# A grouped 1x1 convolution limited by transfers: splitting its relief chunks into two partition-offset variants with buffers and queues of their own

## The chip, the cores and the metric

One core of one Trainium2 chip. The time is that of the device, in microseconds, from many executions. Executions of the kernel before spread from 513.6 to 527.6 us over all rounds, 2.7% from the fastest to the slowest, so comparisons are made between runs of the same rounds on the same chip. A "ratio" below is the mean time of one kernel's fast runs over the mean of the other's fast runs of the same rounds, so it is not quite the ratio of the medians that are quoted beside it. Verdicts are at 2%: a change under 2% is called "same".

## The reference

```python
H = W = 512; G = 4; Cg = 48; C = 192; k = 1        # x: (1, 512, 512, 192) bf16, w: (1, 1, 4, 48, 48) bf16
xg = x.reshape(B, H, W, G, Cg)
out = einsum('bhwgc,gcd->bhwgd', xg, w[0, 0])       # four independent 48x48 products for each pixel
```

262,144 pixels of 384 bytes are read and as many written: 201.3 MB. That is nearly all there is to pay for.

## The kernel before

Pixels are cut into chunks. A natural chunk gives 32 pixels to each of 128 partitions (one partition's share is one run of 12,288 bytes). Four pixels of each partition make a group: TensorE transposes it (six transposes), VectorE copies the result out of PSUM, TensorE multiplies it with a block weight (six matmuls), ScalarE and VectorE copy the product to an output buffer. SyncE issues loads, ScalarE issues stores.

Every fourth chunk is a "relief" chunk of 120 partitions. Its store is issued from GpSimd, behind a tiny transfer of one partition:

```python
RPARTS = 120
nparts = [128 if k == "nat" else RPARTS for k in kinds]
...
# GpSimd, for a relief chunk
gp.dma_start(scratch[0:1, 2 * nd + 1:2 * nd + 2], scratch[0:1, 0:1]).then_inc(dm_sem, 16)
gp.dma_start(rows_view(of, n), o_sb[b][0:RPARTS, 0:F]).then_inc(ra_sem[b], 16)
...
# SyncE, for every chunk: 128 partitions, also for the 120 of a relief chunk
src = xf[chunk_pix0[n]:chunk_pix0[n] + 128 * sizes[n], :].rearrange("(p i) c -> p (i c)", p=128)
sp.dma_start(x_sb[b][:, 0:sizes[n] * C], src).then_inc(ld_sem[b], 16)
```

The plan behind it: a store of 120 partitions is to leave one of the core's sixteen DMA engines without work, and the tiny transfer is to see to it that it is the same one each time. For the first half the trace speaks: each of the sixteen relief stores has sixteen completion marks, one of them 2.8 to 10.4 us ahead of the next (3.1 us against 9.4 and later for the store issued at 398.86 us). Which engine that is, and whether it is always the same, no view shows; that was assumed. Five load buffers and six store buffers serve both kinds of chunk.

## Time and profile before

| | before |
|---|---|
| median time, 4 runs known at the start | 522.45 us (519.64 to 527.58) |
| TensorE busy | 81% |
| bytes moved, mean rate | 203.83 MB, 388 GB/s |
| a load of 128 partitions, issue to landing | 32.8 us |
| TensorE's waits for loads | 88.1 us in 37 waits |

The lines of the page, and how they are read, stand in the prediction below.

### The profile page before, as it was taken

How to read it: one execution, taken by the hardware profiler on the slowest of the kernel's cores; microseconds unless marked ns; L12 is line 12 of the kernel's file. 1: busy time of each engine (PE TensorE's matmuls, PEld its weight loads, DVE VectorE, ACT ScalarE, POOL GpSimd, SP SyncE). 2: the span in 40 equal slices, each digit the busy share in tenths (PEclk: the TensorE clock that was granted, in tenths of full speed). 3: DMA queues.
4: the chain of work that ended last, by engine and by line, in shares of the span. 5: the costliest groups of instructions: out<-in, count | busy, mean ns of one | idle time of the engine just before them, and what ended most of it. 6: DMA issues, size and time to landing. Idle time of an engine off the chain costs nothing.

```text
span 525.6 us, 14096 instructions
## 1 busy us (share of the span) xinstructions
PE 426.9 (81%) x6250; PEld 417.4 (79%) x6250; DVE 352.2 (67%) x677; ACT 351.9 (67%) x521; POOL 18.1 (3%) x41
## 2 busy tenths in 40 slices
PE   4999938499894978989598598977978597887894
PEld 4999937499884977988498597977977596887793
DVE  2788917378673865868477386874867575676783
ACT  2698826468683874868477396874867575776784
POOL 1000000000000000000000000000000000000000
PEclk9999969789897997989989798997999989999999
DMA  8999999999999999999999999999999999999986
GB/s 296 420 396 421 335 419 387 402 401 388 427 398 393 399 392 408 367 415 423 401 403 373 397 354 382 427 403 417 370 423 419 406 412 371 422 351 393 339 311 249
DMA packets 21229, 203.83 MB, mean 388 GB/s; under 512 B 3120, under 2 KB 4144, under 8 KB 5168
## 3 DMA queue, kind: packets, MB, share of 16 engines
q1 hardware_dynamic: 10432, 102.26, 47.5%
q10 hardware_dynamic: 7920, 77.07, 35.9%
q0 software_dynamic: 2816, 23.60, 13.9%
q8 instruction: 49, 0.80, 0.6%
q14 instruction: 12, 0.10, 0.1%
HBM read 102.25 MB, written 100.66 MB: 386 GB/s over the span
## 4 chain that ended last, share of the span: by engine, by line
DMA 66%; PE 31%; SPq 0%; issue 0%; ACT 0%; ACTq 0%
DMA x_sb<-in_x_dram 66%; PE o_ps L279 17%; PE xT_ps L257 15%; SPq L227 0%; ACT o_sb L337 0%; SPq L222 0%; ACTq L322 0%; ACTq L38 0%
## 5 line engine op out<-in xcount | busy, mean ns | idle before, releaser
L304 DVE COPY xT_sb<-xT_ps 128x768 bf16<-128x768 bf16 x520 | 288.1, 555 | 159.2 <-PE xT_ps L257 157.6
L337 ACT CAST o_sb<-o_ps 128x768 bf16<-128x768 f32 x364 | 281.9, 800 | 123.3 <-PE o_ps L279 123.0
L257 PE MATMUL xT_ps<-ident,x_sb 128*128 128x128 bf16 x3120 | 274.9, 227 | 88.9 <-DMA x_sb<-in_x_dram 88.1
L279 PE MATMUL o_ps<-wt,xT_sb 128*128 128x144 bf16 (+1 forms) x3120 | 317.6, 241 | 0.0
L257 PEld LDWEIGHTS xT_ps<-ident,x_sb 128*128 128x128 bf16 x3120 | 211.2, 102 | 97.6 <-DMA x_sb<-in_x_dram 95.6
L279 PEld LDWEIGHTS o_ps<-wt,xT_sb 128*128 128x128 bf16 x3120 | 234.3, 102 | 0.6 <-ACT o_sb L337 0.2
L333 ACT CAST o_sb<-o_ps 128x384 bf16<-128x384 f32 x156 | 74.9, 480 | 43.6 <-PE o_ps L279 42.9
L312 DVE CAST o_sb<-o_ps 128x384 bf16<-128x384 f32 x156 | 86.2, 552 | 3.4 <-PE o_ps L279 2.6
L208 POOL DMA_DIRECT2D scratch<-scratch x16 | 8.3, 520 | 475.7 <-DVE xT_sb L304 421.2
L210 POOL DMA_DIRECT2D out_dram<-o_sb x16 | 8.6, 535 | 0.0
L299 DVE CAST wt<-o_ps 128x480 bf16<-128x480 f32 x1 | 0.7, 657 | 3.4 <-PE o_ps L240 3.4
L240 PE MATMUL o_ps<-w_sb,esel 48*128 48x48 bf16 x10 | 0.6, 210 | 2.8 <-DMA w_sb<-in_w_dram 2.8
L240 PEld LDWEIGHTS o_ps<-w_sb,esel 48*128 48x128 bf16 x10 | 0.5, 110 | 2.7 <-POOL esel L189 2.7
L337 ACT ACT_TABLE_LOAD x1 | 1.3, 1283 | 0.8 <-PEq L363 0.8
L189 POOL TENSOR_SCALAR_AFFINE_SELECT esel<-esel 48x272 bf16<-48x272 bf16 x1 | 0.4, 405 | 0.0
L185 POOL MEMSET esel<- 48x272 bf16 x1 | 0.3, 318 | 0.3 <-POOLq L363 0.3
L193 POOL TENSOR_SCALAR_AFFINE_SELECT ident<-ident 128x128 bf16<-128x128 bf16 x1 | 0.3, 290 | 0.0
L186 POOL MEMSET ident<- 128x128 bf16 x1 | 0.2, 198 | 0.0
L187 POOL MEMSET scratch<- 16x40 bf16 x1 | 0.1, 122 | 0.0
L363 POOL MEMSET const-float32-0.0<- 128x1 f32 x1 | 0.1, 99 | 0.3 <-issue 0.3
L363 POOL MEMSET const-bfloat16-1.0<- 128x1 bf16 x1 | 0.1, 103 | 0.0
L363 POOL MEMSET const-uint8-127<- 128x1 uint8 x1 | 0.1, 102 | 0.0
(1 smaller groups left out, 0.1 us busy)
## 6 DMA issues: line engine op xcount, KB each, us to landing
x_sb<-in_x_dram SPq DMA_DIRECT2D x63, 1536.0 KB, 32.8
out_dram<-o_sb ACTq DMA_DIRECT2D x47, 1536.0 KB, 15.4
out_dram<-o_sb POOLq DMA_DIRECT2D x16, 1440.0 KB, 16.2
x_sb<-in_x_dram SPq DMA_DIRECT2D x2, 768.0 KB, 20.4
out_dram<-o_sb ACTq DMA_DIRECT2D x2, 768.0 KB, 10.6
x_sb<-in_x_dram SPq DMA_DIRECT2D x4, 192.0 KB, 7.5
x_sb<-in_x_dram SPq DMA_DIRECT2D x2, 384.0 KB, 13.9
out_dram<-o_sb ACTq DMA_DIRECT2D x4, 192.0 KB, 7.0
```

What stands on the lines that cost most here:

```text
L189: gp.affine_select(out=esel[:], in_=esel[:], pattern=[[-1, ECOLS]], compare_op=AluOpType.is_equal, fill=0.0, base=ESHIFT, channel_multipli ...
L208: gp.dma_start(scratch[0:1, 2 * nd + 1:2 * nd + 2], scratch[0:1, 0:1]).then_inc(dm_sem, 16)
L210: gp.dma_start(rows_view(of, n), o_sb[b][0:RPARTS, 0:F]).then_inc(ra_sem[b], 16)
L240: last = pe.matmul(o_ps[:, NOB - 1, col:col + 48], lhsT=esel[:, s0:s0 + 128], rhs=w_sb[:, g, :], start=True, stop=True, skip_group_check=True)
L257: last = pe.transpose(xT_ps[:, g % NXP, j * 128:(j + 1) * 128], xb[:, col:col + 128], ident[:])
L279: last = pe.matmul(o_ps[:, v % NOB, c0:c1], lhsT=xs[:, j * 128:(j + 1) * 128], rhs=wt[:, WOFF[tc]:WOFF[tc] + (c1 - c0)], start=(tc == 0), ...
L299: dve.tensor_copy(wt[:], o_ps[:, NOB - 1, 0:WCOLS]).then_inc(dve_done, 1)
L304: dve.tensor_copy(xT_sb[g % NXS][:], xT_ps[:, g % NXP, 0:768]).then_inc(dve_done, 1)
L312: dve.tensor_copy(obuf(n)[:, u * UC:(u + 1) * UC], o_ps[:, v % NOB, 0:UC]).then_inc(dve_done, 1)
L333: ins = act.copy(ob[:, u * UC:(u + 1) * UC], o_ps[:, v % NOB, 0:UC])
L337: ins = act.copy(dst, o_ps[:, v % NOB:v % NOB + 2, 0:UC])
L363: nc = _bacc.Bacc("TRN2", target_bir_lowering=False, num_devices=1)
```

## The change

The intent: relieve DMA engines more, and with finer grain. There are two relief variants, each a range of partitions that does not start at zero: 60 partitions from 36, and 44 partitions from 52. Now their loads too go through GpSimd's queue, into relief buffers of their own, and each transfer has a one-partition or a five-partition transfer ahead of it, which was to decide which engines are relieved (the code's `move_cursor`; the recorded texts speak of the cursor). That such transfers steer anything was an assumption. There are 24 relief chunks instead of 16, so that 620 groups are computed, not 520. Because a relief range ends at partition 96, the transposes of a relief group use 96 rows, and rows below the range hold zeros. The diff, shortened:

```diff
-NBI=5, NBO=6, n_relief=16, first_relief=3, relief_gap=3
-RPARTS = 120
+NBI = 5; NBO = 5; NRI = 2; NRO = 2
+RELIEF = {"relA": (36, 60, 1), "relB": (52, 44, 5)}   # first partition, partitions, tiny transfer's partitions
+REND = 96
+B_EVERY = 4; N_RELIEF = 24; FIRST_RELIEF = 4; RELIEF_GAP = 2
...
+            def move_cursor(skip):
+                gp.dma_start(scratch[0:skip, 2 * nd + 1:2 * nd + 2], scratch[0:skip, 0:1]).then_inc(dm_sem, 16)
+            def load(n):
+                wait_in_free(wq, n)
+                ...
+                move_cursor(skip)
+                gp.dma_start(xr_sb[i][p0_:p0_ + rows, 0:sizes[n] * C], rows_view(xf, n)).then_inc(rl_sem[i], 16)
+            def store(n):
+                wait_evacuated(wq, n)
+                ...
+                move_cursor(skip)
+                gp.dma_start(rows_view(of, n), or_sb[i][p0_:p0_ + rows, 0:sizes[n] * C]).then_inc(rs_sem[i], 16)
...
-            for n in range(n_chunks):                      # SyncE
+            for n in nat_ids:
...
-  pe.transpose(xT_ps[:, g % NXP, j * 128:(j + 1) * 128], xb[:, col:col + 128], ident[:])
+  pe.transpose(xT_ps[:, g % NXP, j * 128:j * 128 + rows], xb[0:rows, col:col + 128], ident[0:rows, 0:rows])
...   (clearing of xr_sb and xT_sb at the start; the copies of relief groups take 96 of 128 columns)
```

More of the change, by code (lines that the diff above doesn't have):

```diff
@@ L7 @@
 F32 = mybir.dt.float32
-C = 192
+GROUPS = 4
+CG = 48
+C = GROUPS * CG
 UC = 2 * C
@@ L20 @@
 ECOLS = 272
+PPC = 32
+HEAD = (4, 4, 8, 16)
+TAIL = (16, 8, 4, 4)
+NBI = 5
+NBO = 5
+NRI = 2
+NRO = 2
 NOB = 5
@@ L24 @@
 LOOK = 2
-RPARTS = 120
+RELIEF = {"relA": (36, 60, 1), "relB": (52, 44, 5)}
+REND = 96
+RPPC = 32
+B_EVERY = 4
+N_RELIEF = 24
+FIRST_RELIEF = 4
+RELIEF_GAP = 2
+SHARE = (2, 4, 7)
+ST_DELAY = 1
 class Waiter:
@@ L38, in wait @@
         self.eng.wait_ge(sem, val)
-def _ints(v):
-    return tuple(int(t) for t in str(v).split("_") if t != "")
-def plan_chunks(npix, PPC, RPPC, n_relief, head, tail, first_relief, relief_gap):
-    assert npix % 128 == 0
-    rel_pix = RPARTS * RPPC
-    while n_relief > 0 and (npix - n_relief * rel_pix) % 512 != 0:
-        n_relief -= 1
-    cols = (npix - n_relief * rel_pix) // 128
-    if n_relief == 0 or cols < sum(head) + sum(tail) + PPC:
-        n_relief = 0
-        cols = npix // 128
-    if cols < sum(head) + sum(tail):
-        head, tail = (), ()
-    mid = cols - sum(head) - sum(tail)
-    nat = list(head)
-    while mid > 0:
-        s = min(PPC, mid)
-        nat.append(s)
-        mid -= s
-    nat += list(tail)
-    assert all(s % 4 == 0 for s in nat)
-    chunks = [("nat", s) for s in nat]
-    pos = first_relief
-    for r in range(n_relief):
-        pos = min(pos, len(chunks) - len(tail))
-        chunks.insert(pos, ("rel", RPPC))
-        pos += relief_gap + 1
-    return chunks
@@ L73, in bass_standalone__grouped__vision_kernel, with relief_kinds, plan_chunks @@
-def bass_standalone__grouped__vision_kernel(nc, x, w, out, PPC=32, NBI=5, NBO=6, head="4_4_8_16", tail="16_8_4_4",
-           share="2_4_7", n_relief=16, first_relief=3, relief_gap=3, st_delay=1, nat_ring="act"):
+def relief_kinds(n_relief):
+    return ["relB" if B_EVERY and i % B_EVERY == B_EVERY - 1 else "relA" for i in range(n_relief)]
+def plan_chunks(npix):
+    assert npix % 512 == 0, "the pixel count must be a multiple of 512"
+    for n_relief in range(N_RELIEF, -1, -1):
+        rk = relief_kinds(n_relief)
+        rest = npix - sum(RELIEF[k][1] * RPPC for k in rk)
+        if rest < 0 or rest % 512 != 0:
+            continue
+        cols = rest // 128
+        head, tail = list(HEAD), list(TAIL)
+        if cols < sum(head) + sum(tail) + PPC:
+            if n_relief:
+                continue
+            head, tail = [], []
+        mid = cols - sum(head) - sum(tail)
+        nat = head
+        while mid > 0:
+            nat.append(min(PPC, mid))
+            mid -= nat[-1]
+        nat += tail
+        chunks = [("nat", s) for s in nat]
+        pos = FIRST_RELIEF
+        for k in rk:
+            pos = min(pos, len(chunks) - len(tail))
+            chunks.insert(pos, (k, RPPC))
+            pos += RELIEF_GAP + 1
+        return chunks
+    raise AssertionError("no chunk plan")
@@ L75, in bass_standalone__grouped__vision_kernel @@
+def bass_standalone__grouped__vision_kernel(nc, x, w, out):
     B, H, W_, Cx = x.shape
-    assert Cx == C
+    assert Cx == C and tuple(w.shape) == (1, 1, GROUPS, CG, CG)
     npix = B * H * W_
-    head, tail, share = _ints(head), _ints(tail), set(_ints(share))
-    chunks = plan_chunks(npix, PPC, PPC, n_relief, head, tail, first_relief, relief_gap)
-    assert chunks[-1][0] == "nat"
+    chunks = plan_chunks(npix)
     n_chunks = len(chunks)
@@ L83, in bass_standalone__grouped__vision_kernel @@
     sizes = [c[1] for c in chunks]
-    assert all(s % 4 == 0 for s in sizes)
-    rel_ids = [n for n in range(n_chunks) if kinds[n] == "rel"]
+    nrows = [128 if k == "nat" else RELIEF[k][1] for k in kinds]
     nat_ids = [n for n in range(n_chunks) if kinds[n] == "nat"]
+    rel_ids = [n for n in range(n_chunks) if kinds[n] != "nat"]
     n_rel = len(rel_ids)
-    ordinal, cnt = {}, {"nat": 0, "rel": 0}
-    for n in range(n_chunks):
-        ordinal[n] = cnt[kinds[n]]
-        cnt[kinds[n]] += 1
-    nparts = [128 if k == "nat" else RPARTS for k in kinds]
+    ordinal = {n: i for ids in (nat_ids, rel_ids) for i, n in enumerate(ids)}
     xf = x.rearrange("b h w c -> (b h w) c")
@@ L100, in bass_standalone__grouped__vision_kernel @@
         chunk_pix0.append(p0)
-        p0 += nparts[n] * sizes[n]
+        p0 += nrows[n] * sizes[n]
     assert p0 == npix
@@ L110, in shared @@
     def shared(g):
-        return (g % 5 == 2) or ((g % 10) in share)
+        return (g % 5 == 2) or ((g % 10) in SHARE)
     dve_prog = [("wcopy", 0)]
@@ L123, in rows_view @@
     def rows_view(ap, n):
-        s = sizes[n]
-        return ap[chunk_pix0[n]:chunk_pix0[n] + nparts[n] * s, :].rearrange("(p i) c -> p (i c)", p=nparts[n])
+        rows, s = nrows[n], sizes[n]
+        return ap[chunk_pix0[n]:chunk_pix0[n] + rows * s, :].rearrange("(p i) c -> p (i c)", p=rows)
     with ExitStack() as es:
@@ L130, in bass_standalone__grouped__vision_kernel @@
         o_sb = [es.enter_context(nc.sbuf_tensor(f"o_sb{i}", [128, PPC * C], BF16)) for i in range(NBO)]
-        xT_sb = [es.enter_context(nc.sbuf_tensor(f"xT_sb{i}", [128, 768], BF16)) for i in range(NXS)]
+        xr_sb = [es.enter_context(nc.sbuf_tensor(f"xr_sb{i}", [128, RPPC * C], BF16)) for i in range(NRI)]
+        or_sb = [es.enter_context(nc.sbuf_tensor(f"or_sb{i}", [128, RPPC * C], BF16)) for i in range(NRO)]
+        xT_sb = [es.enter_context(nc.sbuf_tensor(f"xT_sb{i}", [128, 2 * UC], BF16)) for i in range(NXS)]
@@ L132, in bass_standalone__grouped__vision_kernel @@
         ident = es.enter_context(nc.sbuf_tensor("ident", [128, 128], BF16))
-        esel = es.enter_context(nc.sbuf_tensor("esel", [48, ECOLS], BF16))
-        w_sb = es.enter_context(nc.sbuf_tensor("w_sb", [48, 4, 48], BF16))
+        esel = es.enter_context(nc.sbuf_tensor("esel", [CG, ECOLS], BF16))
+        w_sb = es.enter_context(nc.sbuf_tensor("w_sb", [CG, GROUPS, CG], BF16))
         wt = es.enter_context(nc.sbuf_tensor("wt", [128, WCOLS], BF16))
-        scratch = es.enter_context(nc.sbuf_tensor("scratch", [16, 2 * max(n_rel, 1) + 8], BF16))
+        scratch = es.enter_context(nc.sbuf_tensor("scratch", [16, 4 * max(n_rel, 1) + 8], BF16))
@@ L137, in bass_standalone__grouped__vision_kernel, with sem @@
         xT_ps = es.enter_context(nc.psum_tensor("xT_ps", [128, NXP, 1024], BF16))
         o_ps = es.enter_context(nc.psum_tensor("o_ps", [128, NOB, 512], F32))
-        sem = lambda name: es.enter_context(nc.semaphore(name))
+        def sem(name):
+            return es.enter_context(nc.semaphore(name))
         ld_sem = [sem(f"ld{i}") for i in range(NBI)]
         st_sem = [sem(f"st{i}") for i in range(NBO)]
-        ra_sem = [sem(f"ra{i}") for i in range(NBO)]
-        dm_sem = sem("dm_sem")
@@ L145, in bass_standalone__grouped__vision_kernel @@
-        w_sem, id_sem, e_sem, p0_sem, p1_sem, sc_sem = (sem(n_) for n_ in ("w_sem", "id_sem", "e_sem", "p0_sem", "p1_sem", "sc_sem"))
-        wb_sem = sem("wb_sem")
-        t_done, mm_done, dve_done, act_done = sem("t_done"), sem("mm_done"), sem("dve_done"), sem("act_done")
+        rl_sem = [sem(f"rl{i}") for i in range(NRI)]
+        rs_sem = [sem(f"rs{i}") for i in range(NRO)]
+        z_sem = sem("z_sem")
+        zt_sem = sem("zt_sem")
+        w_sem, id_sem, e_sem, wb_sem = sem("w_sem"), sem("id_sem"), sem("e_sem"), sem("wb_sem")
@@ L150, in xbuf, with used_rows @@
+        p0_sem, p1_sem, sc_sem, dm_sem = sem("p0_sem"), sem("p1_sem"), sem("sc_sem"), sem("dm_sem")
+        t_done = sem("t_done")
+        mm_done = sem("mm_done")
+        dve_done = sem("dve_done")
+        act_done = sem("act_done")
         def xbuf(n):
-            return x_sb[n % NBI]
+            return x_sb[ordinal[n] % NBI] if kinds[n] == "nat" else xr_sb[ordinal[n] % NRI]
+        def used_rows(n):
+            return 128 if kinds[n] == "nat" else REND
         def obuf(n):
-            return o_sb[n % NBO]
@@ L156, in bass_standalone__grouped__vision_kernel, with wait_loaded @@
-        st_before, nat_c, rel_c = {}, [0] * NBO, [0] * NBO
-        for n in range(n_chunks):
-            st_before[n] = (nat_c[n % NBO], rel_c[n % NBO])
+            return o_sb[ordinal[n] % NBO] if kinds[n] == "nat" else or_sb[ordinal[n] % NRO]
+        def wait_loaded(wq, n):
+            k = ordinal[n]
             if kinds[n] == "nat":
-                nat_c[n % NBO] += 1
+                wq.wait(ld_sem[k % NBI], 16 * (k // NBI + 1))
             else:
-                rel_c[n % NBO] += 1
@@ L164, in wait_loaded @@
-        def wait_loaded(wq, n):
-            wq.wait(ld_sem[n % NBI], 16 * (n // NBI + 1))
+                wq.wait(rl_sem[k % NRI], 16 * (k // NRI + 1))
         def wait_in_free(wq, n):
-            if n >= NBI:
-                wq.wait(t_done, chunk_g1[n - NBI])
-        def wait_out_free(wq, n):
-            a_, r_ = st_before[n]
-            wq.wait(st_sem[n % NBO], 16 * a_)
-            wq.wait(ra_sem[n % NBO], 16 * r_)
+            k = ordinal[n]
+            if kinds[n] == "nat":
+                if k >= NBI:
+                    wq.wait(t_done, chunk_g1[nat_ids[k - NBI]])
+            elif k >= NRI:
+                wq.wait(t_done, chunk_g1[rel_ids[k - NRI]])
@@ L176, in wait_evacuated @@
+        def wait_out_free(wq, n):
+            k = ordinal[n]
+            if kinds[n] == "nat":
+                wq.wait(st_sem[k % NBO], 16 * (k // NBO))
+            else:
+                wq.wait(rs_sem[k % NRO], 16 * (k // NRO))
         def wait_evacuated(wq, n):
@@ L196, in _ @@
             gp.wait_ge(sc_sem, 1)
-            nd = 0
-            for n in range(n_chunks):
-                b = n % NBO
-                if kinds[n] == "nat" and nat_ring != "pool":
-                    continue
-                wait_evacuated(wq, n)
-                F = sizes[n] * C
-                if kinds[n] == "nat":
-                    if nat_ring == "pool":
-                        gp.dma_start(rows_view(of, n), o_sb[b][:, 0:F]).then_inc(st_sem[b], 16)
-                else:
-                    gp.dma_start(scratch[0:1, 2 * nd + 1:2 * nd + 2], scratch[0:1, 0:1]).then_inc(dm_sem, 16)
-                    nd += 1
-                    gp.dma_start(rows_view(of, n), o_sb[b][0:RPARTS, 0:F]).then_inc(ra_sem[b], 16)
@@ L211, in _ @@
-            for b in range(NBO):
-                if nat_c[b] and nat_ring == "pool":
-                    gp.wait_ge(st_sem[b], 16 * nat_c[b])
-                if rel_c[b]:
-                    gp.wait_ge(ra_sem[b], 16 * rel_c[b])
-            if nd:
-                gp.wait_ge(dm_sem, 16 * nd)
+            state = {"nd": 0}
+            def move_cursor(skip):
+                nd = state["nd"]
+                gp.dma_start(scratch[0:skip, 2 * nd + 1:2 * nd + 2], scratch[0:skip, 0:1]).then_inc(dm_sem, 16)
+                state["nd"] = nd + 1
@@ new lines, in load @@
+            def load(n):
+                wait_in_free(wq, n)
+                i = ordinal[n] % NRI
+                p0_, rows, skip = RELIEF[kinds[n]]
+                move_cursor(skip)
+                gp.dma_start(xr_sb[i][p0_:p0_ + rows, 0:sizes[n] * C], rows_view(xf, n)).then_inc(rl_sem[i], 16)
+            def store(n):
+                wait_evacuated(wq, n)
+                i = ordinal[n] % NRO
+                p0_, rows, skip = RELIEF[kinds[n]]
+                move_cursor(skip)
+                gp.dma_start(rows_view(of, n), or_sb[i][p0_:p0_ + rows, 0:sizes[n] * C]).then_inc(rs_sem[i], 16)
@@ new lines, in _ @@
+            for i in range(1, NRI if n_rel else 0, 2):
+                gp.memset(xr_sb[i][:], 0.0).then_inc(z_sem, 1)
+            if n_rel:
+                gp.wait_ge(z_sem, NRI)
+            for n in rel_ids[:NRI]:
+                load(n)
+            for k, n in enumerate(rel_ids):
+                store(n)
+                if k + NRI < n_rel:
+                    load(rel_ids[k + NRI])
+            for i in range(NRO):
+                cnt = len(rel_ids[i::NRO])
+                if cnt:
+                    gp.wait_ge(rs_sem[i], 16 * cnt)
@@ L219, in _ @@
+            if state["nd"]:
+                gp.wait_ge(dm_sem, 16 * state["nd"])
         @block.sync
@@ L222, in _ @@
             sp.dma_start(w_sb[:], wv).then_inc(w_sem, 16)
-            for n in range(n_chunks):
+            for n in nat_ids:
                 wait_in_free(wq, n)
-                b = n % NBI
-                src = xf[chunk_pix0[n]:chunk_pix0[n] + 128 * sizes[n], :].rearrange("(p i) c -> p (i c)", p=128)
-                sp.dma_start(x_sb[b][:, 0:sizes[n] * C], src).then_inc(ld_sem[b], 16)
+                b = ordinal[n] % NBI
+                sp.dma_start(x_sb[b][:, 0:sizes[n] * C], rows_view(xf, n)).then_inc(ld_sem[b], 16)
         @block.tensor
@@ L239, in build_weights, with transposes @@
                     col = WOFF[tc] + c0
-                    last = pe.matmul(o_ps[:, NOB - 1, col:col + 48], lhsT=esel[:, s0:s0 + 128], rhs=w_sb[:, g, :],
-                                     start=True, stop=True, skip_group_check=True)
+                    last = pe.matmul(o_ps[:, NOB - 1, col:col + CG], lhsT=esel[:, s0:s0 + 128],
+                                     rhs=w_sb[:, g, :], start=True, stop=True, skip_group_check=True)
                 last.then_inc(wb_sem, 1)
-            def T(g):
+            def transposes(g):
                 n, lg = groups[g]
@@ L250, in T @@
                 xb = xbuf(n)
+                rows = used_rows(n)
                 last = None
@@ L256, in T, with matmuls @@
                         j = ul * 3 + tc
-                        last = pe.transpose(xT_ps[:, g % NXP, j * 128:(j + 1) * 128], xb[:, col:col + 128], ident[:])
+                        last = pe.transpose(xT_ps[:, g % NXP, j * 128:j * 128 + rows],
+                                            xb[0:rows, col:col + 128], ident[0:rows, 0:rows])
                 last.then_inc(t_done, 1)
-            def MM(g):
+            def matmuls(g):
                 xs = xT_sb[g % NXS]
@@ L272, in MM @@
                         wq.wait(dve_done, need)
-                    else:
-                        if g >= 2:
-                            wq.wait(act_done, act_cnt[g - 2])
+                    elif g >= 2:
+                        wq.wait(act_done, act_cnt[g - 2])
                     for tc in range(3):
@@ L285, in _ @@
             for g in range(min(LOOK, NG)):
-                T(g)
+                transposes(g)
             for g in range(NG):
                 if g + LOOK < NG:
-                    T(g + LOOK)
-                MM(g)
+                    transposes(g + LOOK)
+                matmuls(g)
         @block.vector
@@ L294, in _ @@
             wq = Waiter(dve)
+            for i in range(NXS if n_rel else 0):
+                dve.memset(xT_sb[i][:], 0.0).then_inc(zt_sem, 1)
+            if n_rel:
+                dve.wait_ge(zt_sem, NXS)
             waited_chunk = -1
-            for (kind, g) in dve_prog:
-                if kind == "wcopy":
+            for (op, g) in dve_prog:
+                if op == "wcopy":
                     wq.wait(wb_sem, 1)
@@ L301, in _ @@
                 n, lg = groups[g]
-                if kind == "ev1":
+                if op == "ev1":
                     wq.wait(t_done, g + 1)
-                    dve.tensor_copy(xT_sb[g % NXS][:], xT_ps[:, g % NXP, 0:768]).then_inc(dve_done, 1)
+                    rows = used_rows(n)
+                    src = xT_ps[:, g % NXP, 0:2 * UC].rearrange("p (j c) -> p j c", c=128)[:, :, 0:rows]
+                    dst = xT_sb[g % NXS][:].rearrange("p (j c) -> p j c", c=128)[:, :, 0:rows]
+                    dve.tensor_copy(dst, src).then_inc(dve_done, 1)
                 else:
@@ L311, in _ @@
                     v = 2 * g + 1
-                    dve.tensor_copy(obuf(n)[:, u * UC:(u + 1) * UC], o_ps[:, v % NOB, 0:UC]).then_inc(dve_done, 1)
+                    dve.tensor_copy(obuf(n)[:, u * UC:(u + 1) * UC],
+                                    o_ps[:, v % NOB, 0:UC]).then_inc(dve_done, 1)
         @block.scalar
@@ L316, in _, with store @@
             wq = Waiter(act)
-            pend = []
-            def issue_store(n):
+            for i in range(0, NRI if n_rel else 0, 2):
+                act.memzero(xr_sb[i][:]).then_inc(z_sem, 1)
+            pending = []
+            def store(n):
                 wait_evacuated(wq, n)
-                b = n % NBO
+                b = ordinal[n] % NBO
                 act.dma_start(rows_view(of, n), o_sb[b][:, 0:sizes[n] * C]).then_inc(st_sem[b], 16)
@@ L338, in _ @@
                 ins.then_inc(act_done, 1)
-                if nat_ring == "act":
-                    if g == chunk_g1[n] - 1 and kinds[n] == "nat":
-                        pend.append((n, g + st_delay))
-                    while pend and pend[0][1] <= g:
-                        issue_store(pend.pop(0)[0])
-            if nat_ring == "act":
-                for (n, _) in pend:
-                    issue_store(n)
-                for b in range(NBO):
-                    if nat_c[b]:
-                        act.wait_ge(st_sem[b], 16 * nat_c[b])
+                if g == chunk_g1[n] - 1 and kinds[n] == "nat":
+                    pending.append((n, g + ST_DELAY))
+                while pending and pending[0][1] <= g:
+                    store(pending.pop(0)[0])
+            for (n, _) in pending:
+                store(n)
+            for b in range(NBO):
+                cnt = len(nat_ids[b::NBO])
+                if cnt:
+                    act.wait_ge(st_sem[b], 16 * cnt)
 _INS = ['x', 'w']
```

## The prediction

> **What bounds the kernel now.** I read the page from the top: engine shares, the 40 slices, the queues, the chain; then the waits, the issues and stretches of the tensor engine's timeline.
>
> ```profile
> PE 426.9 (81%) x6250; PEld 417.4 (79%) x6250; DVE 352.2 (67%) x677; ACT 351.9 (67%) x521; POOL 18.1 (3%) x41
> ...
> DMA  8999999999999999999999999999999999999986
> GB/s 296 420 396 421 335 419 387 402 401 388 427 398 393 399 392 408 367 415 423 401 403 373 397 354 382 427 403 417 370 423 419 406 412 371 422 351 393 339 311 249
> DMA packets 21229, 203.83 MB, mean 388 GB/s; under 512 B 3120, under 2 KB 4144, under 8 KB 5168
> ## 3 DMA queue, kind: packets, MB, share of 16 engines
> q1 hardware_dynamic: 10432, 102.26, 47.5%
> q10 hardware_dynamic: 7920, 77.07, 35.9%
> q0 software_dynamic: 2816, 23.60, 13.9%
> q8 instruction: 49, 0.80, 0.6%
> ...
> DMA x_sb<-in_x_dram 66%; PE o_ps L279 17%; PE xT_ps L257 15%; SPq L227 0%; ACT o_sb L337 0%; SPq L222 0%; ACTq L322 0%; ACTq L38 0%
> ...
> x_sb<-in_x_dram SPq DMA_DIRECT2D x63, 1536.0 KB, 32.8
> out_dram<-o_sb ACTq DMA_DIRECT2D x47, 1536.0 KB, 15.4
> out_dram<-o_sb POOLq DMA_DIRECT2D x16, 1440.0 KB, 16.2
> ```
> DMA is 9 in nearly every slice; two thirds of the chain is loads; a load needs 32.8 us from issue to landing, a store of the same size 15.4. The best slices reach 427 GB/s, the mean is 388, and the last three slices fall to 339, 311, 249. So the bound is DMA, at 91% of its own best rate.
>
> ```profile
> PE xT_ps L257 <- DMA x_sb<-in_x_dram: 88.1, 37, 8.0
> ...
> 30.92 0.58 PE L279 MATMUL o_ps<-wt,xT_sb 128*128 128x144 bf16 x6
> ...
> 31.67 0.58 PE L279 MATMUL o_ps<-wt,xT_sb 128*128 128x144 bf16 x6
> ...
> 106.13 0.84 PE L257 MATMUL xT_ps<-ident,x_sb 128*128 128x128 bf16 x6
> ...
> 107.57 0.84 PE L257 MATMUL xT_ps<-ident,x_sb 128*128 128x128 bf16 x6
> ```
> The tensor engine waits 37 times for a load, 88.1 us in all. Fed, it makes a group (six transposes, six matmuls) every 31.67 - 30.92 = 0.75 us; just after a wait, at half clock, every 107.57 - 106.13 = 1.44 us. 520 groups x 0.75 = 390 us is its floor.
>
> Why do loads take twice as long as stores? The trace holds the sixteen completion marks of each transfer. For the load issued at 415.55 us, fifteen fall between 9.1 and 14.1 us after issue and the sixteenth at 37.9; for the one at 270.39, 6.0 to 12.4 and 32.3. All later loads look so: **one of the sixteen DMA engines is some 20 us behind.** In the first 200 us two to five lag (160.41: 21.5, 24.0, 25.4 and 39.2 close the list).[...]
>
> [...] in each old relief store one mark comes far ahead of the rest (3.1 us against 9.4 and later at 398.86), the engine with nothing to move.
> [...] of the 12,288-byte packets in the hardware queues 80% take 0.46 us and 90% under 0.48; of those in the software queue 20% take over 0.78 and 10% over 0.96.
>
> **The change part by part.**
> *Chunks.* The planner finds 24 relief chunks (18 of 60 partitions, 6 of 44) and 428 natural groups: 428 + 24 x 8 = 620 groups, up from 520.
> *Bytes.* Relief loads now read their own rows; before they read 128 partitions for 120. Saved: 16 x 8 x 12,288 B = 1.57 MB of 203.83, or 3.7 us at 427 GB/s.
> *DMA engine by engine* (a packet is one partition of a chunk, 12,288 B, 0.46 us). Before: loads 102.26/16 = 6.39 MB, natural stores 77.07/16 = 4.82, relief 23.60/15 = 1.57. Spared engine 11.21 MB = 912 packets, others 12.78 MB = 1040. After: natural 219,136 pixels x 384 B x 2 / 16 = 10.52 MB = 856 packets[...].
> *The laggard.* 912 x 0.46 = 420 us would not lag. Something else sits there, and the q8 line offers it: 49 packets of 16 KB, 0.94 us each, 46 us. 0.80 MB over 12,500 PE instructions is 64 B each, so I take this to be PE's program on one engine's ring. The laggard then has (520 - 46)/912 = 0.52 us a packet.[...] After: PE has 620 x 24 = 14,880 instructions, so 58 fetches, 54.5 us; 856 packets at 0.48 to 0.52 give 411 to 445; sum 466 to 500, middle 483.[...]
> *PE.* A relief group transposes 96 rows, not 128: 6 x 32 columns less. Six natural transposes take 0.75 - 0.42 = 0.33 us of the pace, so a quarter off is 0.08 and the group 0.67. 428 x 0.75 + 192 x 0.67 = 450 us, up from 390. Off the path, but only just.
> *ACT and DVE.* ACT: (281.9 + 74.9) x 620/520 = 425 us. DVE: 428 x 0.555 + 192 x about 0.44 (576 of 768 columns) + 186 x 0.552 = 425. Neither bounds.
> *GpSimd.* 96 issues at about 0.53 us, 51 us over the span. Relief loads go out two relief chunks ahead, about 40 us: hidden.
> *Start.* Clearing the two relief inputs delays the first relief load to an estimated 8 us; its chunk is the fifth and is wanted near 17 us. 0 to 3 us.
> *Sum.* Middle stage: three chunks (two natural, one relief) cost a full engine 40 packets, 18.4 us, plus overhead 18.8; PE 16 x 0.75 + 8 x 0.70 = 17.6. Twenty-four cycles 451, the 5.5 natural chunk sizes outside them at about 8 us 44, the end stage less 2 to 3. With start and drain I get **497 us**, 5% less. Cross-check: 202.3 MB (fetches included) at 415 GB/s, near the good slices, is 487, plus about 10 of ramp and drain.
>
> **The rivals.**
> *PE becomes the bound.* For it: 100 groups more, and half clock after each wait; 88 us of waits shrink to about 30. Against: 450 is still 35 us under DMA, and fewer long waits mean fewer cold restarts. If it won, 505 to 515.
> *The laggard stays.* More fetches and 0.54 us or worse a packet: 856 x 0.56 + 54 = 533, the same or slower. For it: the cause of the 0.52 is partly unexplained. Against: it loses 56 packets[...].
> *Software-queue cost.* 33.0 MB instead of 23.6 through the queue whose packets were slow. If slowness belongs to the queue and not to the partitions, some 2,700 packets at about 0.1 us more spread over 16 engines cost 17 us: about 510.
> *Gap rounds to nothing.* If the 7% below 427 GB/s is contention and not imbalance, only 3.7 us of bytes go: 518.
>
> **Range and chances.** Before is 522.45, its runs 519.6 to 527.6; 2% faster is 512.0. The balanced floor is about 484 (482 plus start), so I put the low end at 486; the rivals at 505 to 515 set the high end, 512. Faster 0.82, same 0.15, slower 0.03.
>
> **What would show it.** Right: load landing falls from 32.8 to under 25 us; the sixteenth mark closes up to the others; mean rate over 400 GB/s; PE waits for loads fall below 45 us; relief packets at 0.46 us like the rest. Wrong: one mark still 20 us behind (laggard), PE idle near zero with DMA slices at 8 (PE bound), software packets still over 0.7 us for a fifth of them (queue cost), new waits of PE on the relief inputs. The estimate falls if the long fetch packets are not on the engine that lags.

The 482 us in it is the author's estimate for the fullest engines, 1,048 packets of 0.46 us. Like the 40 packets of the sum, it assumes a spread of the relief rows over the engines that no trace had shown. An even sixteenth of a queue's bytes for each engine, there and below, is an estimate, too: the packets of a trace name no engine.

## The result and the profile after

| | before | after |
|---|---|---|
| median | 522.87 us (16 runs) | 527.48 us (11 runs) |
| ratio | 1 | 1.0088 (95% interval 1.0057 to 1.0119) |

A little slower (under 2%, so the verdict is "same"), where 497 us had been predicted. A word on the profiled executions: that of the kernel before took 527.58 us, the slowest of its first four and 1.5% over the fastest, and is for that reason called slow; that of the changed kernel took 528.68 us and is called fast. The profile of the kernel before with a probe in it, taken at 523.71 us, moves 402 to 403 GB/s in the middle, so the views of before may show some 5 GB/s too little. No conclusion below hangs on that difference; the verdicts are those of the timed rounds.

First the page of the changed kernel.

```profile
PE 468.6 (89%) x7450; PEld 458.2 (87%) x7450; DVE 399.8 (76%) x810; ACT 412.2 (78%) x622; POOL 55.5 (11%) x106
...
GB/s 297 281 418 381 389 419 395 398 390 413 382 391 399 413 395 372 414 399 399 415 397 382 417 378 405 417 387 382 417 390 399 417 379 375 416 417 416 373 306 137
DMA packets 22744, 202.43 MB, mean 384 GB/s; under 512 B 4624, under 2 KB 5648, under 8 KB 6928
...
DMA out_dram<-o_sb 60%; PE o_ps L322 14%; PE xT_ps L300 10%; DMA x_sb<-in_x_dram 10%; DMA xr_sb<-in_x_dram 2%; POOL xr_sb L246 1%; ACT o_sb L390 1%; ACT o_sb L386 0%; POOL scratch L228 0%; POOL esel L216 0%; POOL esel L212 0%; POOL ident L2
...
x_sb<-in_x_dram SPq DMA_DIRECT2D x51, 1536.0 KB, 39.1
out_dram<-o_sb ACTq DMA_DIRECT2D x51, 1536.0 KB, 39.5
```

1.40 MB fewer are moved, but the mean rate is 384 GB/s instead of 388. Loads did not get quicker (39.1 us, 32.8 before), and stores have become as slow as loads (39.5, 15.4 before). The chain consists mostly of stores (60% of the span), where it had consisted of loads (66%). The second slice stands out: 281 GB/s, where the kernel before had 420.

The longest waits of the changed kernel (engine and tile, what ended the wait: us in all, number, longest):

```profile
ACT o_sb L390 <- DMA out_dram<-o_sb: 21.0, 14, 3.0
...
PE xT_ps L300 <- DMA x_sb<-in_x_dram: 22.6, 20, 3.3
...
PE o_ps L322 <- ACT o_sb L390: 15.0, 9, 2.3
...
PE xT_ps L300 <- DMA xr_sb<-in_x_dram: 6.8, 1, 6.8
```

TensorE's waits for loads did fall, from 88.1 to 22.6 us, as predicted. It has more groups to work on, so this is not a gain: time to wait in has been filled with the hundred extra groups. New are waits of ScalarE for store buffers, and one of 6.8 us for the first relief load.

By stage, before and after (window, length, busy time and instructions of each engine, granted clock, DMA share, GB/s):

```profile
0.00:24.00 24.00, 16.98 (x193) 16.21 (x194) 11.08 (x21) 10.10 (x14) 1.44 (x10) 1.00 0.91 351
24.00:200.00 176.00, 142.29 (x2117) 140.18 (x2114) 118.99 (x230) 119.18 (x177) 6.33 (x12) 0.91 1.00 398
200.00:494.00 294.00, 245.32 (x3607) 239.82 (x3606) 203.01 (x390) 201.87 (x300) 9.92 (x20) 0.93 1.00 397
```

```profile
0.00:24.00 24.00, 12.33 (x131) 11.35 (x132) 8.85 (x18) 9.43 (x10) 8.81 (x14) 0.86 0.92 292
24.00:200.00 176.00, 171.51 (x2823) 169.95 (x2822) 150.01 (x305) 154.53 (x235) 20.32 (x40) 1.00 1.01 397
200.00:494.00 294.00, 264.99 (x4251) 258.55 (x4248) 227.17 (x463) 233.05 (x356) 26.42 (x52) 0.99 1.00 399
```

The middle stage moves 397 to 399 GB/s in both kernels. The start lost (351 - 292) GB/s x 24 us = 1.4 MB, which cancels the 1.40 MB saved. So the question is: why 397 to 399 in the middle, while the DMA share is at 1.00? The trace lists each packet with its length. The mean of the 12,288-byte packets is 493 ns before (487 in the probed profile) and 494 ns after, against a median of 460. What changed is which packets are long:

| packets of 12,288 B longer than 500 ns | before | after |
|---|---|---|
| load queue of SyncE | 5% | 21% |
| store queue of ScalarE | 6% | 15% |
| relief queue of GpSimd | 30% (22% in the probed profile) | 26% |

The slowness had been said to belong to the relief packets. It spread to everybody's.

The second thing to look at: the sixteen completion marks of a transfer (the trace has sixteen times for each; they are read as one for each DMA engine). In the changed kernel the load issued at 259.38 us has marks at 10.7, then from 30.1 to 39.5, and the last at 42.7 us. Read so, one engine is far ahead, and the fifteen others land 30 to 43 us after the issue; every load issued between 60 and 440 us has one such early mark, at least 7.2 us ahead of the next. And every relief transfer, of 60 or of 44 rows, shows exactly one mark ahead of the others, by 4.3 to 16.6 us after the first transfer, where it is 1.8 us (the load of 44 rows at 49.11 us: 3.3, then 16.7 to 18.6). By the plan five marks of a 44-row transfer should have been early. That did not fit the prediction and gave the first rival theory.

### The profile page after: what moved, and what is told of

Its sections match the earlier page's. It is cut to its first block, busy times and chain, and to the rows that moved or that the text cites. A ratio compares the mean times of both kernels' runs of the same rounds, so it can differ in the third digit from the quotient of the medians.

```text
span 527.0 us, 16823 instructions
## 1 busy us (share of the span) xinstructions
PE 468.6 (89%) x7450; PEld 458.2 (87%) x7450; DVE 399.8 (76%) x810; ACT 412.2 (78%) x622; POOL 55.5 (11%) x106
## 4 chain that ended last, share of the span: by engine, by line
DMA 72%; PE 25%; POOL 1%; ACT 1%; issue 0%; POOLq 0%; ACTq 0%
DMA out_dram<-o_sb 60%; PE o_ps L322 14%; PE xT_ps L300 10%; DMA x_sb<-in_x_dram 10%; DMA xr_sb<-in_x_dram 2%; POOL xr_sb L246 1%; ACT o_sb L390 1%; ACT o_sb L386 0%; POOL scratch L228 0%; POOL esel L216 0%; POOL esel L212 0%; POOL ident L220 0%; POOL ident L213 0%; POOL scratch L214 0%; ACTq L57 0%
## 5 line engine op out<-in xcount | busy, mean ns | idle before, releaser
L354 DVE COPY xT_sb<-xT_ps 128x768 bf16<-128x768 bf16 (+1 forms) x620 | 320.3, 524 | 97.7 <-PE xT_ps L300 94.8
L322 PE MATMUL o_ps<-wt,xT_sb 128*128 128x144 bf16 (+1 forms) x3720 | 368.6, 235 | 21.2 <-ACT o_sb L390 15.0
L390 ACT CAST o_sb<-o_ps 128x768 bf16<-128x768 f32 x300 | 230.4, 801 | 74.2 <-PE o_ps L322 51.4
L322 PEld LDWEIGHTS o_ps<-wt,xT_sb 128*128 128x128 bf16 x3720 | 263.7, 99 | 26.6 <-ACT o_sb L390 17.2
L300 PE MATMUL xT_ps<-ident,x_sb 128*128 128x128 bf16 x2568 | 216.9, 221 | 22.8 <-DMA x_sb<-in_x_dram 22.6
L300 PEld LDWEIGHTS xT_ps<-ident,x_sb 128*128 128x128 bf16 x2568 | 166.3, 99 | 27.2 <-DMA x_sb<-in_x_dram 26.4
L390 ACT CAST or_sb<-o_ps 128x768 bf16<-128x768 f32 x134 | 101.5, 804 | 9.9 <-PE o_ps L322 6.8
L300 PE MATMUL xT_ps<-ident,xr_sb 96*128 96x96 bf16 x1152 | 82.1, 207 | 6.8 <-DMA xr_sb<-in_x_dram 6.8
L386 ACT CAST o_sb<-o_ps 128x384 bf16<-128x384 f32 x128 | 61.8, 483 | 25.9 <-PE o_ps L322 13.3
L300 PEld LDWEIGHTS xT_ps<-ident,xr_sb 96*128 96x128 bf16 x1152 | 65.1, 98 | 7.1 <-DMA xr_sb<-in_x_dram 7.0
L362 DVE CAST or_sb<-o_ps 128x384 bf16<-128x384 f32 x58 | 32.2, 555 | 0.7
## 6 DMA issues: line engine op xcount, KB each, us to landing
x_sb<-in_x_dram SPq DMA_DIRECT2D x51, 1536.0 KB, 39.1
out_dram<-o_sb ACTq DMA_DIRECT2D x51, 1536.0 KB, 39.5
```

The costliest lines, as they stand in the source:

```text
L300: last = pe.transpose(xT_ps[:, g % NXP, j * 128:j * 128 + rows], xb[0:rows, col:col + 128], ident[0:rows, 0:rows])
L322: last = pe.matmul(o_ps[:, v % NOB, c0:c1], lhsT=xs[:, j * 128:(j + 1) * 128], rhs=wt[:, WOFF[tc]:WOFF[tc] + (c1 - c0)], start=(tc == 0), ...
L354: dve.tensor_copy(dst, src).then_inc(dve_done, 1)
L362: dve.tensor_copy(obuf(n)[:, u * UC:(u + 1) * UC], o_ps[:, v % NOB, 0:UC]).then_inc(dve_done, 1)
L386: ins = act.copy(ob[:, u * UC:(u + 1) * UC], o_ps[:, v % NOB, 0:UC])
L390: ins = act.copy(dst, o_ps[:, v % NOB:v % NOB + 2, 0:UC])
```

## The experiments

**Theory A**, from the prediction: one DMA engine lags because it also carries TensorE's program, and relief spares it. **Theory B**: the lagging engine is another one. **A shared ceiling**: mixed loads and stores cannot exceed about 398 GB/s, whatever the balance. The later **theories C and D** differ in whether the tiny transfers steer anything.

### Which engine lags: a probe in both kernels

Fifteen tiny loads, of 1, 2, ... 15 partitions, are put into SyncE's queue behind big ones, at two places of the run. The ladder is read by its step: the k at which the latest mark of a list jumps, against the list of k - 1. The engine numbers in the expectations are the author's names for such steps (k - 1 for a step at k, 15 for none); which engines of the chip they are, no view shows.

```diff
+                if ordinal[n] in (25, 40):          # in the kernel before: n in (32, 52)
+                    for k in range(1, 16):
+                        c = k + (16 if ordinal[n] == 40 else 0)
+                        sp.dma_start(probe[0:k, 64 * c:64 * c + 64], xf[0:k, 0:64]).then_inc(pr_sem[k], 16)
+            for k in range(1, 16):
+                sp.wait_ge(pr_sem[k], 32)
```

> The kernel before with fifteen tiny loads of 1 to 15 partitions put into the load queue behind two big loads[...]. Theory A (the engine that the relief spares[...] is the laggard because it carries PE's program fetches): the very first tiny load, k = 1, is already about 20 us late. Theory B (the laggard is one of the engines that the relief does not spare): k = 1 comes early and a late mark of 10 to 20 us more appears at some higher k[...].

> The same probe in the changed kernel. Theory A: engine 0 late. Theory B: [...] the one latest mark lies at the same engine number as in the kernel before, 5 or higher.

Measured: 523.71 us and 533.97 us, one run each (the second is some 6 us over the unprobed kernel; the probe itself disturbs). The latest marks of neighbouring lists, in us from the start of the run:

| | latest mark of the list of k - 1 | of the list of k | step at k |
|---|---|---|---|
| before, first place | 218.4 (list of 9) | 234.8 (list of 10) | 10 |
| before, second place | 377.6 (list of 9) | 390.9 (list of 10) | 10 |
| after, first place | 210.0 (list of 4) | 212.9 (list of 5) | 5, by under 3 us: not clearly apart |
| after, second place | 356.9 (list of 4) | 374.2 (list of 5) | 5 |

Theory A expected the list of one partition to be late already. In none of the four is it the latest; the late mark comes with the list of 10, or of 5. Theory A, as its expectations put it, is out. The step is at 10 in one program and at 5 in the other, so the laggard keeps no one place of the ladder either. For the kernel before this is what theory B expected; for the changed kernel the expectation (the same step as before) was missed.

The first place of the changed kernel shows more. There the list of one partition, which stood for the engine that the relief was to spare, was as far behind as the others: it was issued at 173.79 us and marked at 204.6, 30.8 us later. The big load just ahead of the lists (issued at 173.42 us) has one mark after 6.0 us and fifteen from 29.0 to 38.5. All fifteen lists were late, so none of them shows the engine of the early mark; the author took it for one that the ladder does not reach, called 15, and not for the one of the plan. No view names it.

### Transfers alone

64 natural loads and 64 stores of the same bytes, ten buffers, no compute; the output is x itself, wrong on purpose. The second of the two kernels also runs 4,200 matmuls on TensorE that depend on nothing. Both carry the probe, which is left out here, as are a few waits.

```python
for n in range(N):                                   # SyncE
    if n >= NB: sp.wait_ge(st[n % NB], 16 * (n // NB))
    sp.dma_start(x_sb[n % NB][:], rows_view(xf, n)).then_inc(ld[n % NB], 16)
for n in range(N):                                   # ScalarE
    act.wait_ge(ld[n % NB], 16 * (n // NB + 1))
    act.dma_start(rows_view(of, n), x_sb[n % NB][:]).then_inc(st[n % NB], 16)
for i in range(PE_N):                                # TensorE: 4, or 4,200
    last = pe.matmul(o_ps[:, i % 4, 0:256], lhsT=ident[:, 0:128], rhs=ident[:, 0:256], ...)
```

> Only the transfers: 64 loads of 128 partitions and 64 stores of the same bytes, no compute (its output is x, wrong on purpose), with the probe. If each DMA engine has its own limit of 0.46 us a packet and imbalance is what costs: 1024 packets x 0.46 = 471 us plus start and drain, about 480 us, marks of a load close together. If a shared ceiling holds mixed loads and stores to about 398 GB/s: 506 us plus start, about 512 us, with packets over 0.46 us. If a laggard shows here too, it is not PE's program fetch.

> The transfers alone, as in the quiet copy (476 us), but beside them 4,200 independent matmuls on TensorE, whose program takes about 33 fetches of 16 KB. If PE's program fetch makes the laggard: one mark of each load, at one engine number in the probe, falls behind by up to 33 x 0.95 = 31 us, and the whole takes about 20 to 31 us longer than 476. If the laggard has another cause: as the quiet copy, within 3 us.

Measured: 476.37 us quiet and 485.26 us with TensorE at work (one run each). The rates of the two, in forty slices:

```profile
GB/s 306 431 431 431 431 431 429 430 431 429 430 431 428 431 431 430 431 431 419 430 431 431 431 430 431 431 428 430 429 422 431 430 430 429 430 431 429 430 431 341
```

```profile
GB/s 311 426 427 428 428 428 427 429 428 428 428 427 429 429 426 430 425 421 420 428 428 428 429 425 431 425 430 425 422 425 426 429 426 430 426 429 430 425 380 202
```

Loads and stores together hold 431 GB/s: there is no ceiling at 398. That theory is out. In the quiet copy the marks of a load lie within about 2 us of each other in the middle of the run (load at 200.31 us: 51.2 to 53.3); beside TensorE one mark is some 4 us behind the others (280.87 us: fifteen from 48.0 to 55.4, one at 59.7), and at the second place of the probe one mark of the list of 5 is the last (356.3 us, the next mark 349.8). So beside TensorE's work one mark lags and the copy takes 8.9 us longer, 485.26 against 476.37 us. Theory A expected 20 to 31 us of 33 program fetches, its rival at most 3; neither came true. The page of the second copy has 33 packets of 16 KB on q8 (0.54 MB), that of the quiet one none; that they are the cause of the late mark is not shown.

### Ranges and tiny transfers, changed together and one by one

Theory D is the plan of the change: the tiny transfers decide which engines take the relief rows, and the ranges from 36 and 52 suit that. Theory C: the tiny transfers steer nothing, and the first partition of a range is what counts; from 32 a relief transfer should cost less than from 36 or 52. The author's reason for 32 was an assumption on how the rows are spread; no run shows it. What the runs can tell apart is the effect of the first partition and that of the tiny transfers.

```diff
-RELIEF = {"relA": (36, 60, 1), "relB": (52, 44, 5)}
+RELIEF = {"relA": (32, 60, 1), "relB": (32, 44, 5)}   # spare_last, shift_only, no_cursor
 
-                move_cursor(skip)                       # spare_last, cursor_only: moved behind; no_cursor: removed
                 gp.dma_start(...)                       # the relief load, and the relief store
+                move_cursor(skip)                       # spare_last, cursor_only
```

First both, as a test of theory B (the intent was to spare the engine called 15 instead of the one called 0):

> The changed kernel, but the relief uses partitions 32 to 91 and 32 to 75 and the cursor is moved after the transfer[...]. If the laggard is engine 15 (or any of 11 to 15, in part): the late mark of the loads closes up, the end stage shortens by about 8 us, ratio to before about 0.985 to 0.995. If the laggard is among 1 to 10, or if a shared ceiling near 398 GB/s is all that counts: within 0.5% of the changed kernel, ratio 1.005 to 1.012. If it is engine 0: slower than the changed kernel by 2% or more.

Then one at a time, and without tiny transfers:

> The changed kernel with the relief ranges moved to start at partition 32 (32-91 and 32-75), cursor moves still ahead of the transfers. Theory C (the one-partition transfers don't steer[...]): as fast as the kernel that changed both, ratio to before about 0.976. Theory D (the cursor steers as planned[...]): [...] no faster than the changed kernel, ratio 1.005 to 1.015.

> The changed kernel with its ranges 36-95 and 52-95 kept and the cursor moved after each transfer. Theory C: nothing changes, ratio to before 1.005 to 1.012 as in the changed kernel. Theory D with the spared engine as the cause: as fast as the kernel that changed both, 0.976, or between.

> Ranges from partition 32 and no cursor-moving transfers at all. Theory C: as fast as with them, 0.970 to 0.978. Theory D: [...] ratio 1.00 or more.

| kernel | first partition | tiny transfers | median | before, same rounds | ratio (95%) |
|---|---|---|---|---|---|
| the change | 36 / 52 | ahead | 527.48 | 522.87 | 1.0088 (1.0057 to 1.0119) |
| cursor_only | 36 / 52 | behind | 527.83 | 521.56 | 1.0095 (1.0032 to 1.0158) |
| spare_last | 32 / 32 | behind | 508.08 | 520.09 | 0.9756 (0.9689 to 0.9824) |
| shift_only | 32 / 32 | ahead | 507.97 | 521.56 | 0.9717 (0.9665 to 0.9770) |
| no_cursor | 32 / 32 | none | 506.75 | 521.56 | 0.9693 (0.9630 to 0.9755) |

By verdict the change and cursor_only are the same as before, shift_only and no_cursor faster, spare_last unclear (its interval reaches 0.9824).

Only the first partition matters: moved to 32 it takes some 20 us off (527.48 to 507.97 us with the tiny transfers ahead, 527.83 to 508.08 with them behind); the place of the tiny transfers matters not at all, and leaving them out gains about a microsecond (507.97 to 506.75). This is theory C on every line, and D on none. It also shows that spare_last, which lay outside all three of its expectations, was not fast for the reason it was built for (its laggard was not spared either: its load at 479.63 us has fifteen marks by 6.4 us and one at 18.9).

The stages of shift_only and then of cursor_only, columns as above:

```profile
0.00:24.00 24.00, 13.56 (x145) 12.88 (x146) 9.37 (x19) 10.23 (x11) 8.80 (x14) 0.86 0.91 355
24.00:200.00 176.00, 176.00 (x2919) 175.54 (x2917) 154.93 (x315) 159.75 (x243) 20.32 (x40) 1.00 1.01 416
```

```profile
0.00:24.00 24.00, 13.51 (x139) 12.83 (x140) 9.09 (x19) 10.06 (x11) 8.80 (x14) 0.88 0.92 284
24.00:200.00 176.00, 173.86 (x2835) 173.03 (x2834) 151.30 (x307) 155.54 (x237) 20.50 (x40) 0.99 1.01 398
```

The same DMA share, 1.01, carries 416 GB/s in one and 398 in the other. So the time that the starts at 36 and 52 cost is counted as busy. The loss of the start (284 and 355 GB/s) goes with the first partition, too. With the ranges from 32, TensorE is busy for all 176 us of the second stage: the extra groups now bound it there.

### A dose, and the 44-row chunks

If the start costs by its distance from 32, and not by any start other than 32, ranges that start at 34 should cost about half of what the change does. And if the 44-row chunks are dear even from 32, a kernel with 60-row chunks alone should be 3 to 6 us faster, otherwise within 1 us.

```diff
-RELIEF = {"relA": (36, 60, 1), "relB": (52, 44, 5)}
+RELIEF = {"relA": (34, 60, 1), "relB": (34, 44, 5)}   # off_half; otherwise as the change

-B_EVERY = 4                                            # all_a: no_cursor with
+B_EVERY = 0                                            #   60-row chunks only
```

> The changed kernel with both ranges starting at partition 34[...]. [...] half way between the range at 32 (508 us) and the change (527.5), so 515 to 520, ratio to before 0.985 to 0.995. [...] as the change, 1.005 to 1.012. If the start at 32 is fast for another reason (a power of two, say): also as the change.

> No cursor moves, every relief chunk of the 60-row kind, from partition 32. [...] 3 to 6 us faster than the 507 with them, ratio about 0.96. [...] no faster, within 1 us of 507.

Measured: off_half 516.67 us, ratio 0.9906 (0.9845 to 0.9966), inside the 515 to 520 expected and half way between 508 and 527.5 (by verdict "same" as before, since it is under 2%). all_a 502.18 us, ratio 0.9633 (0.9568 to 0.9699), 4.6 us under no_cursor, also as expected. So a start at 34 lies between those at 32 and at 36 and 52, and the kernel with 44-row chunks takes longer than that with 60-row ones in their place (506.75 against 502.18 us).

The packets of the five kernels beside their times (relief packets are counted from the ranges, loads and stores both; the change's trace has 2,688 packets of 12,288 bytes in GpSimd's queue):

| kernel | first partitions | relief packets | mean length of all 12,288-byte packets | median time |
|---|---|---|---|---|
| the change | 36 / 52 | 18 x 60 x 2 + 6 x 44 x 2 = 2,688 | 494 ns | 527.5 |
| off_half | 34 / 34 | 2,688 | 480 ns | 516.7 |
| shift_only | 32 / 32 | 2,688 | 472 ns | 508.0 |
| no_cursor | 32 / 32 | 2,688 | 472 ns | 506.8 |
| all_a | 32, 60-row chunks alone | 24 x 60 x 2 = 2,880 | 466 ns | 502.2 |

From the change to off_half it is 10.8 us and 14 ns, from there to shift_only 8.7 us and 8 ns, from no_cursor to all_a 4.6 us and 6 ns, with 192 relief packets more. The kernels ran in different rounds; worked out from the ratios of their own rounds, at 522 us, the three steps are 9.5, 9.9 and 3.1 us, and for the last of them the intervals of the two ratios overlap. The times fall with the mean length of the packets. Why packets are longer in the kernels whose ranges start past 32, or that have 44-row chunks, is in no record.

### No relief at all

```diff
-N_RELIEF = 24
+N_RELIEF = 0          # no_relief: the changed kernel

-    ... n_relief=16, first_relief=3, ...
+    ... n_relief=0, first_relief=3, ...      # before_no_relief: the kernel before
```

In the first of the two texts "aligned" stands for ranges from 32, and 15 is the name from the ladder. The second asks whether the relief's rows are what held the kernel before at 397 GB/s.

> The changed kernel without any relief chunk: 512 groups, all rows natural, GpSimd issues nothing, 1024 packets on every engine. If sparing engine 15 is worth something by itself: slower than the aligned relief, 512 to 520. If the lagging engine is another one than 15, the aligned relief only adds packets to it and work to PE: as fast or faster, 497 to 508, ratio 0.955 to 0.975.

> The kernel before with its sixteen relief chunks taken away and nothing else: five load and six store buffers, all natural. [...] like the changed kernel without relief, 491 to 497 us, ratio 0.940 to 0.952, and the load marks within about 5 us of each other in the middle stage. If its lagging engine had another cause and the relief helped against it: slower than 522 us. If the dedicated buffers or the five store buffers of the change are worth something: in between, 500 to 510.

Measured: no_relief 493.64 us, ratio 0.9458 (0.9405 to 0.9512); before_no_relief 492.01 us, ratio 0.9510 (0.9410 to 0.9610; it was called unclear, because one run of the kernel before was at 513.6 us in these rounds, so that four of its seven runs counted as slow). Both results are correct. no_relief is faster than either of its expectations (497 to 508 us at best). The page of no_relief:

```profile
PE 401.0 (82%) x6154; PEld 386.0 (79%) x6154; DVE 342.2 (70%) x666; ACT 340.9 (69%) x513; POOL 1.4 (0%) x9
...
GB/s 306 421 408 427 425 424 429 429 425 425 424 428 429 428 424 428 428 427 425 426 428 427 428 423 427 427 428 427 426 428 427 426 425 427 428 428 425 364 310 137
...
x_sb<-in_x_dram SPq DMA_DIRECT2D x62, 1536.0 KB, 30.2
```

A level 425 to 428 GB/s. Packets have a mean of 464 ns, and in the middle the marks of a load lie together (203.25 us: 21.8 to 28.2, the last at 30.2). The 20 us laggard of the kernel before is gone from the middle stage without being spared; in before_no_relief the load at 196.12 us has its marks from 23.3 to 30.7 and 32.1 (a spread of 8.8 us, where about 5 was expected). A smaller one comes back in the second half: in no_relief the last mark trails the one before it by a median of 0.4 us in loads issued between 60 and 200 us, by 4.7 us between 200 and 440 us, and by 8 us at the end, when the load at 462.33 us has fifteen marks by 11.1 us and the last at 19.0. This end, below 400 GB/s in the last three slices, is most of what still separates 493 from the 476 of the quiet copy.

So the relief was worth less than nothing in both kernels. Even the best one, that of all_a, costs 8.5 us against none. An estimate from the counts, with the 60 rows spread evenly over fifteen engines, as the one early mark in sixteen of the change suggests: 24 x 2 x 4 = 192 relief packets and 422 natural groups x 2 make 1,036 packets there instead of 1,024, 12 x 0.46 = 5.5 us. The rest is not settled (102 extra groups, a later start). Of the dedicated relief buffers these two kernels say nothing, since without relief chunks no transfer uses them; what they compare is five store buffers with six (493.6 and 492.0 us). No run tests the relief buffers alone.

The best kernels of this study are thus the two without relief, 5.4% and 4.9% under the kernel before by the ratios of their own rounds.

## Why the prediction was wrong, point by point

**The bound** (DMA, at 91% of its best rate): right. The kernel before reached 492 us once its transfers ran level.

**The laggard is the spared engine, and carries PE's program**: wrong, as far as the ladder tells. Its late mark came with the list of 10 before and of 5 after, and nowhere with that of one partition; in the changed kernel the list of one partition was not even early (31 us behind like the rest, at 173.79 us). The prediction saw one late mark in loads and one early mark in relief stores and took them for the same engine, with nothing in the trace to say so. There was a sign against it: in the kernel before, the last mark of a relief store is often late, too (at 464.11 us fourteen marks from 6.5 to 10.1 us, one at 13.6), so the laggard may have taken part in the relief. That a mark lags beside TensorE's work was in part right: 9 us in the copy with matmuls.

**That tiny transfers steer**: the spread of the relief rows, and the balance with it, rested on this, and it is the step that failed. They steer nothing that shows (527.83 against 527.48 us, 506.75 with none against 507.97). One mark in sixteen is early in the 60-row and in the 44-row transfers, where the plan had one and five. It was an assumption, and no run had tested it before.

**Where the ranges start**: the author took 36 and 52 for the better place, by assumption. The runs say the opposite: from 36 and 52 the kernel takes 527.48 us, from 34 516.67, from 32 507.97. The kernel before, whose relief stores start at partition 0 with 120 rows, lost 30.6 us against its version without relief. That also holds 1.57 MB of surplus loads and eight more groups; what of it is due to the relief's rows was not tested.

**Engine by engine** (1,048 packets on the fullest, by estimate): wrong for the same reason. One mark was early in both variants, and not four more in the 44-row one. The balance that was to give 18.8 us a cycle did not come about.

**PE**: right. Relief groups take 25.15 - 24.48 = 0.67 us in the chain of the changed kernel, as worked out. (The sum of the middle stage counted 0.70 for it; that slip makes 0.2 us a cycle and did not matter, since DMA was the larger term.) The half clock that one rival expected "after each wait" came less often: in the profile of the kernel before, 12 of TensorE's 37 pauses over 0.3 us were followed by a granted clock of 0.50, among them all eight longer than 3.5 us. TensorE did not bound the whole run, but with the ranges from 32 it fills the second stage (176.00 of 176.00 us), so there was less room than "just off the path" suggests.

**VectorE, GpSimd**: right in size. The 96-column copy took 455 ns (0.44 predicted), an issue of GpSimd 0.51 to 0.53 us; relief loads were hidden, except the first.

**Start**: 0 to 3 us predicted, 6.8 us of waiting measured. The clearing ended as estimated (first relief load at 8.2 us), but that load took 11.9 us, and TensorE wanted it at 13.3 us, not near 17.

**The rivals**: "the laggard stays" and "the gap rounds to nothing" each had a part of the picture. The first was right that a laggard remained. The second was right that no more than the bytes would be gained, for a reason it did not have: the gap came with the relief itself; without it both kernels move 424 to 427 GB/s between 24 and 470 us, against 397 to 399 with it. "Software-queue cost" supposed that slowness stays with the slow packets; instead load packets over 500 ns went from 5% to 21%. That the first partition of one stream goes with longer packets in the others was on no list.

**What stays open**: how relief rows are spread over the engines, and why a start at 32 is faster than one at 34, or at 36 and 52; why one mark is late beside TensorE's work, and why the ladder's step is at 10 in one program and at 5 in another. In the last loads of every version of the convolution (issued after 440 us) the last mark trails the one before it, by a median of 3 us (cursor_only) to 15 us (before); what that costs in run time was not measured.

## What to carry to other kernels

Before you balance load over DMA engines, test that your steering steers: here tiny transfers ahead, behind or left out made 1.3 us of difference at most. Completion marks have no names; a ladder of tiny transfers of 1 to 15 partitions can at least tell two programs apart (the late mark came with the list of 10 in one and of 5 in the other). Try a transfer of less than 128 partitions from another first partition: 32 instead of 36 and 52 was worth 20 us here, and the share of busy time was 1.01 with the fast start (416 GB/s) as with the slow one (398 GB/s). And test a workaround against its absence: here the kernel without any relief was the fastest, in both its old and its new form.
